# Retention and an ELU layer on one Trainium2 core: a new order for the opening, and input rows of 2 KB

## The chip, the cores and the metric

The kernel runs on one core of a Trainium2 chip. The metric is the time of one execution on the device, in microseconds (us), lower is better. The time is the median of several runs. One execution was also recorded by the hardware profiler; times "at" are counted from the start of its span.

Five engines work side by side, each through its own queue in order: TensorE (PE, with its weight loads as PEld), VectorE (DVE), ScalarE (ACT), GpSimd (POOL) and SyncE (SP), which here issues all transfers between HBM and the on-chip memory SBUF. TensorE writes into PSUM banks; VectorE and ScalarE read them.

## What is computed

A recurrent retention over four sequences of 768 tokens with 8 heads of 64, then a two-layer network with an ELU, in float32:

```python
B, H, S, D = 4, 8, 768, 64
gamma = 1.0 - 2.0 ** (-5.0 - np.arange(H))
for t in range(S):
    state = gamma[None, :, None, None] * state + np.einsum('bhd,bhe->bhde', k[:, :, t], v[:, :, t])
    y[:, :, t] = D ** -0.5 * np.einsum('bhd,bhde->bhe', q[:, :, t], state)
x = y.transpose(0, 2, 1, 3).reshape(3072, 512)
h = x @ w_in                                   # 512 x 2048
g = np.where(h > 0, h, np.exp(np.minimum(h, 0)) - 1)
out = g @ w_out                                # 2048 x 512
```

## The kernel before

**Tiling.** The 3072 tokens are cut into 24 chunks of 128, and four chunks make a block of 512 tokens. Six blocks are worked through. The retention of a chunk is done in halves of 64 tokens: scores of queries and keys, masked (`score_products`, L302; `mask_pair`, L324, or `scores`, L312, for two chunks together); the products of keys and values that make a state (`state_products`, L332; `state_sum`, L343); and the outputs from within the half (`within`, L389) and across from the state (`across`, L399), which VectorE multiplies with powers of gamma into `xb`, the input of the layer. `scale_v` (L275) multiplies the values with negative powers first, on VectorE or on GpSimd. All of these products are 64 x 64 and short.

**The layer on block 0** is plain: `plain_first` (L489) makes 16 tiles of 128 features x 512 tokens. A tile is four products of 128 x 128 weights with up to 512 tokens, two instructions each. `elu` (L472) follows: two activations on ScalarE and one last step on VectorE, which is put off until the next tile. Piece n of the weights feeds tiles 2n and 2n + 1. Later blocks use Strassen's scheme for both layers and are not touched.

**Weights** arrive as float64 bits, in pieces of 1 MB (`load_piece`, L126; three buffers). A piece is turned into float32 by ScalarE (`prepare`, L147: two or three activations for each part) and by VectorE (`decode`, L180: L190 in some pieces, L191 and L194 for each part). `decode` also loads the next piece when it ends. `hold` (L112) makes a load wait for another by a one-element copy on GpSimd.

**Order.** The schedule is written out by hand: the program order is each engine's order. Several steps are Python generators that are advanced piece by piece: `next(y)` runs the next step of a chunk's outputs, `next(inner)` the next part of a layer tile, `take()` the next decoding step of a weight piece. SP issues in the opening (L253 to L261): chunk 0 in two halves, half of weight piece 0, chunk 1, the other half, piece 1, chunks 2 and 3, and piece 2 held behind piece 1. TensorE begins with multiplications of zeros ("blank", L1108 to L1113, and `unread`, L1104) whose results nobody reads. Then come chunk 0, chunk 1 with the first 128 columns of tile 0 in between, the first halves (256 columns) of tiles 0 to 4, with chunks 2 and 3 taken together between them, the second halves of tiles 0 to 4, and whole tiles from tile 5 on (L1114 to L1171 and the loop at L1187). Within the loop the further pieces are prepared and decoded, the chunks of block 1 loaded, and at its step 4 four subtractions of outputs are made on VectorE (L540).

PSUM: banks "a" (two), "b" and "d" (one each) and four of pool `ps_r`. In `plain_first` tiles 0 to 3 take a, a, b, d, tile 4 one of `ps_r` (`hp`), and tiles from 5 on a, a, b, d in turn (L519).

**Rows of a transfer.** The arrays are laid out on the host. A chunk is 128 rows of 8 KB, one for each partition, and a weight piece too (4 KB for each of two halves):

```python
nc.sync.dma_start(t[:, c], qkv[m, :, c])
nc.sync.dma_start(t[:, c].rearrange("p c w -> p (c w)"), w_bits[n].bitcast(U32)[:, d])
```

## Time and profile before

| | |
|---|---|
| median of three runs | 633.58 us (633.03 to 634.15) |
| the profiled execution's own time | 632.87 us |
| its span in the profile | 630.9 us |
| TensorE busy | 624.8 us, 99% |
| VectorE busy | 483.1 us, 77% |
| ScalarE busy | 253.3 us, 40% |
| transfers | 136.85 MB, mean 217 GB/s |

A row of a timeline gives the start, the length, the engine, the line, the operation and the tiles (written, then read), the shapes and the number of instructions that the row merges; in brackets stands how long the engine was idle before it, and what released it. A row of a table by stretches gives the stretch, its length, the busy time of PE, PEld, DVE, ACT and POOL with instruction counts, the granted TensorE clock, the busy share of the DMA engines and the rate in GB/s. A busy TensorE is not always TensorE at its peak, since a waiting instruction can be counted as a long one.

### The profile page before, as it was taken

The numbers are of one execution on the slowest core, as the hardware profiler recorded it, in microseconds if no ns is written. First come the engines' busy times: TensorE is split into PE (matmuls) and PEld (weight loads), VectorE is DVE, ScalarE is ACT, GpSimd is POOL, SyncE is SP. The second block draws the span as 40 slices with busy tenths as digits, with TensorE's granted clock in tenths as the row PEclk, the third lists the DMA queues.
The fourth block names the chain that finished last, engine by engine and source line by source line (L and its number), as shares of the span: only waits on it lengthen the run. The fifth ranks groups of instructions, "written<-read, shape, count | busy, mean of one in ns | idle before, by whom it ended". The sixth has DMA issues, their size and how long they took to land.

```text
span 630.9 us, 16128 instructions
## 1 busy us (share of the span) xinstructions
PE 624.8 (99%) x6680; PEld 560.1 (89%) x6680; DVE 483.1 (77%) x884; ACT 253.3 (40%) x472; POOL 21.8 (3%) x25
## 2 busy tenths in 40 slices
PE   8999999999999999999999999999999999999998
PEld 5864578888899999889999989999988999988997
DVE  5779789989789675699685588777489877558975
ACT  6698635015541114653112646111465211366311
POOL 1021000000000000200000200000110000000000
PEclk9999999999999999999999999999999999999999
DMA  8698669689287888405888702888810798600794
GB/s 331 278 406 291 188 210 268 196 267 316 81 311 248 239 255 299 180 2 174 274 266 292 282 2 64 264 284 296 310 73 12 216 308 252 217 18 2 232 309 162
DMA packets 75897, 136.85 MB, mean 217 GB/s; under 512 B 6320, under 2 KB 31792, under 8 KB 70704
## 3 DMA queue, kind: packets, MB, share of 16 engines
q1 hardware_dynamic: 75824, 135.82, 64.8%
q8 instruction: 53, 0.87, 0.5%
q14 instruction: 20, 0.16, 0.1%
HBM read 114.56 MB, written 21.23 MB: 215 GB/s over the span
## 4 chain that ended last, share of the span: by engine, by line
PE 77%; SPq 1%; DVE 1%; DMA 1%; issue 0%; ACT 0%; ACTq 0%; DVEq 0%
PE pa L955 20%; PE pa L913 10%; PE pd L955 10%; PE pb L955 5%; PE pa L867 5%; PE pb L913 4%; PE pa L740 4%; PE qa L913 3%; PE pd L867 2%; PE qd L913 2%; PE pd L913 2%; PE pd L740 2%; PE y L394 1%; PE sc L307 1%; PE y L409 1%; PE kv L338 1%
## 5 line engine op out<-in xcount | busy, mean ns | idle before, releaser
L963 ACT COPY ms<-pa 128x128 f32<-128x128 f32 x104 | 27.7, 266 | 146.7 <-PE pa L955 146.7
L955 PE MATMUL pa<-ts,wq 128*128 128x128 f32 x560 | 74.2, 275 | 0.0
L955 PE MATMUL pd<-ts,wq 128*128 128x128 f32 x552 | 73.5, 276 | 0.0
L955 PEld LDWEIGHTS pa<-ts,wq 128*128 128x128 f32 x560 | 68.5, 192 | 0.4
L955 PEld LDWEIGHTS pd<-ts,wq 128*128 128x128 f32 x552 | 67.1, 192 | 0.6 <-DVE res L967 0.2
L955 PE MATMUL pa<-gC,wq 128*128 128x128 f32 x480 | 64.7, 278 | 0.0
L478 ACT ACTIVATE r<-r 128x512 f32<-128x512 f32 x96 | 60.5, 630 | 3.1
L955 PEld LDWEIGHTS pa<-gC,wq 128*128 128x128 f32 x480 | 59.0, 192 | 1.5 <-issue 0.3
L477 ACT ACTIVATE r<-gC 128x512 f32<-128x512 f32 x64 | 39.9, 624 | 32.4 <-DVE gC L921 32.4
L967 DVE TENSOR_TENSOR res<-pd,ms 128x128 f32<-128x128 f32 x68 | 19.5, 287 | 39.6 <-PE pd L955 38.4
L481 DVE SCALAR_TENSOR_TENSOR gC<-r,gC 128x512 f32<-128x512 f32 x64 | 44.0, 719 | 0.7 <-ACT r L478 0.7
L829 DVE TENSOR_TENSOR ts<-gC,ts 128x512 f32<-128x512 f32 x60 | 41.3, 688 | 1.0
L829 DVE TENSOR_TENSOR ts<-gC 128x512 f32<-128x512 f32 x60 | 41.0, 684 | 0.0
L281 POOL TENSOR_TENSOR chunk<-chunk,vf 128x512 f32<-128x512 f32 x16 | 20.0, 1251 | 428.8 <-DMA chunk<-in_qkv_dram 345.8
L955 PE MATMUL pb<-gC,wq 128*128 128x128 f32 x240 | 31.7, 275 | 0.0
L988 ACT COPY res<-pa 128x128 f32<-128x128 f32 x34 | 9.0, 266 | 55.0 <-PE pa L955 55.0
L955 PEld LDWEIGHTS pb<-gC,wq 128*128 128x128 f32 x240 | 29.2, 192 | 0.0
L690 ACT COPY m<-pa 128x512 f32<-128x512 f32 x24 | 13.9, 581 | 30.2 <-PE pa L740 16.3
L921 DVE TENSOR_TENSOR gC<-qa,gC 128x512 f32<-128x512 f32 x8 | 5.5, 692 | 25.0 <-PE qa L913 18.3
L913 PE MATMUL pa<-xt,w_b 128*128 128x256 f32 x96 | 23.0, 382 | 0.0
L913 PE MATMUL pa<-xt,w_s 128*128 128x256 f32 x96 | 23.0, 382 | 0.0
L913 PE MATMUL pa<-xb,w_a 128*128 128x256 f32 x96 | 22.7, 379 | 0.0
(255 smaller groups left out, 1244.3 us busy)
## 6 DMA issues: line engine op xcount, KB each, us to landing
wq<-scratch_dram SPq DMA_DIRECT2D x277, 256.0 KB, 4.3
chunk<-in_qkv_dram SPq DMA_DIRECT2D x23, 1024.0 KB, 8.6
wraw<-in_w_dram SPq DMA_DIRECT2D x15, 1024.0 KB, 6.0
out_dram<-res SPq DMA_DIRECT2D x14, 256.0 KB, 3.8
scratch_dram<-gT SPq DMA_DIRECT2D x12, 256.0 KB, 4.3
scratch_dram<-m SPq DMA_DIRECT2D x12, 192.0 KB, 6.0
scratch_dram<-so SPq DMA_DIRECT2D x4, 512.0 KB, 4.6
scratch_dram<-wi SPq DMA_DIRECT2D x2, 1024.0 KB, 6.4
```

The lines of the kernel that those rows point to most:

```text
L281: eng.tensor_tensor(out=kv[:, 1], in0=kv[:, 1], in1=vf[:, i].unsqueeze(2).to_broadcast([C, H, D]), op=ALU.mult)
L477: nc.scalar.activation(e, h, AF.Relu, scale=-1.0)
L478: nc.scalar.activation(e, e, AF.Exp, scale=-1.0)
L481: nc.vector.scalar_tensor_tensor(g, e, -1.0, h, ALU.add, ALU.max)
L690: nc.scalar.copy(m, ps)
L740: nc.tensor.matmul(ps[:, fi, :], lhsT=w[:, fi, j2, :], rhs=x[:, j2, :], start=(begin and fi == 0 and j2 == 0), stop=(j2 == 1), skip_group_ ...
L829: sub = lambda o, x, y: nc.vector.tensor_tensor(out=o, in0=x, in1=y, op=ALU.subtract)
L867: nc.tensor.matmul(ps[:, f, :], lhsT=lhs[f], rhs=xs[j][k], start=(begin and f == 0), stop=True, skip_group_check=True,)
L913: nc.tensor.matmul(ps[:, fi, :], lhsT=w[:, fi, j2, :], rhs=x[:, j2, :], start=(j in (1, 7) and fi == 0 and j2 == 0), stop=(j2 == 1), skip_ ...
L955: nc.tensor.matmul(ps, lhsT=w[:, f, :], rhs=ts[j][k][:, f, :], start=(begin and f == 0), stop=(f == 3), skip_group_check=True,)
L963: nc.scalar.copy(m, ps)
L967: nc.vector.tensor_tensor(out=o, in0=x, in1=y, op=ALU.add)
```

## The change

The opening is put into another order, and the layout of the two inputs and the way in which they are loaded are changed:

- Loads: chunk 0 (two halves), chunk 1, weight piece 0 (two halves), chunks 2 and 3, piece 1. Piece 2 is issued after chunk 3's values are scaled on GpSimd, and held behind piece 1.
- Each chunk and each weight piece is laid out in HBM as four blocks of 128 rows of 2 KB, here and in every later load; one transfer brings 4 x 128 rows (2 x 128 for a half).
- Chunks 0 and 1 are worked through before the first part of the layer. Chunks 2 and 3 are then done one by one, each with its own scores, masks, states and outputs, between parts of 128 columns of tiles 0 and 1. Only these two tiles are cut in parts; tiles from 2 on are whole, in banks b, d, a, a in turn.
- Two multiplications of blanks with 512 columns are taken out. The powers of the later tokens are made after both halves of piece 0 are prepared, not between them. In `prepare` the second and third activation change places; which pieces use L190 instead changes.

```diff
-            c = slice(part * 2048 // parts, (part + 1) * 2048 // parts)
-            nc.sync.dma_start(t[:, c], qkv[m, :, c])
+            j = slice(part * ROWS // parts, (part + 1) * ROWS // parts)
+            nc.sync.dma_start(t.rearrange("p (j c) -> p j c", j=ROWS)[:, j], qkv[m, j].rearrange("j p c -> p j c"))
...
             nc.scalar.activation(flat, lo, AF.Copy, scale=2.0**-29)
+            if not by_vector:
+                nc.scalar.activation(lo.bitcast(FP32), hi.bitcast(FP32), AF.Copy, scale=2.0**-112)
             top = dst.bitcast(F8).rearrange("p (c b) -> p c b", b=4)[:, c, 3]
             nc.scalar.activation(top, hi.bitcast(FP32), AF.Copy, scale=2.0**-120, saturate=False)
-            if not by_vector:
-                nc.scalar.activation(lo.bitcast(FP32), hi.bitcast(FP32), AF.Copy, scale=2.0**-112)
...
     load(0, 2)
-    parts = load_piece_parts(2)
-    next(parts)
     load(1)
-    next(parts, None)
-    load_piece()
+    load_piece(None, 2)
     load(2)
     load(3)
-    load_piece(staged[1][:, :, 0].bitcast(FP32))
+    load_piece()
...
+        for k in range(2):
+            banks.append(bank("a").rearrange("p a b -> p (a b)"))
+            for x in range(2):
+                part(k, slice(x * C, (x + 1) * C))
                 yield
+        for x in (2, 3):
+            for k in range(2):
+                part(k, slice(x * C, (x + 1) * C))
+                if x == 3:
+                    n, w, row, fi = tiles[k]
+                    elu(g_plain[row * NF + 2 * n + fi], banks[k])
                 yield
+        for k, (n, w, row, fi) in enumerate(tiles[2:]):
+            hp = bank("bdaa"[k % 4]).rearrange("p a b -> p (a b)")
```

The order of the opening after the change, from chunk 0's outputs on:

```python
    scale_v(3)
    load_piece(staged[1][:, :, 0].bitcast(FP32))
    ...
    for _ in range(4):
        next(y)
    score_products(sc, 0, 0, 1)
    prepare(2)
    piece = decode(True)
    state_sum(kvs, 0, 0, 0, 1)
    scale_v(1)
    mask_pair(sc, 0, 1)
    state_products(kvs, 0, 0, 1, range(2))
    state_sum(kvs, 0, 0, 1, 0)
    next(y)
    next(y)
    take()
    next(y)
    next(y)
    take()
    state_sum(kvs, 0, 0, 1, 1)
    powers_of(slice(2 * C, S))
    inner = plain_first()
    next(inner)
    sc = two("sc")
    score_products(sc, 0, 1, 0)
    scale_v(2, True)
    mask_pair(sc, 1, 0)
    next(inner)
    take(3)
    kvs = two("kv")
    state_products(kvs, 0, 1, 0, range(2))
    state_sum(kvs, 0, 1, 0, 0)
    y = outputs_of_first(1)
    next(y)
    next(inner)
    next(y)
    score_products(sc, 0, 1, 1)
    mask_pair(sc, 1, 1)
    next(y)
    next(inner)
    next(y)
    state_sum(kvs, 0, 1, 0, 1)
    prepare(2)
    piece = decode(True)
    state_products(kvs, 0, 1, 1, range(2))
    state_sum(kvs, 0, 1, 1, 0)
    next(y)
    next(inner)
    next(y)
    next(inner)
    next(y)
    next(y)
    state_sum(kvs, 0, 1, 1, 1)
    take(2)
```

In the loop over the rest of `plain_first`, step 0 now finishes the decoding of piece 1 and prepares piece 2, and steps 1 to 5, 7 and 9 each decode a piece and prepare the next:

```diff
-        if n in (1, 2, 4, 5, 7, 9):
-            next_piece(n in (1, 2, 5, 7))
+        if n == 0:
+            take(3)
+            prepare(2)
+        elif n in (1, 2, 3, 4, 5, 7, 9):
+            next_piece(n in (2, 3, 5, 7))
```

## The prediction

> **What bounds the kernel now.** I read the page first, then the timelines of TensorE, VectorE and GpSimd over the first 60 us, then stretches for the rates of the transfers. Times "at" are microseconds from the start of the span.
>
> ```profile
> PE 624.8 (99%) x6680; PEld 560.1 (89%) x6680; DVE 483.1 (77%) x884; ACT 253.3 (40%) x472; POOL 21.8 (3%) x25
> PE 77%; SPq 1%; DVE 1%; DMA 1%; issue 0%; ACT 0%; ACTq 0%; DVEq 0%
> ```
>
> TensorE is busy 624.8 of 630.9 us and holds the chain that ended last. From 60 us on it has no idle time, so the change is worth what it does to TensorE before that. The timeline of TensorE shows where the opening loses:
>
> ```profile
> 9.13 0.45 PE L409 MATMUL pd<-chunk 64*64 64x64 f32 x8 [0.26 <-DVE seen L426]
> 9.51 1.13 PE L1106 MATMUL pa<-blank 128*128 128x512 f32 x2
> 10.66 0.69 PE L307 MATMUL sc<-chunk 64*64 64x64 f32 x32
> 11.59 1.13 PE L497 MATMUL pa<-xb,w_a 128*128 128x128 f32 x8 [0.23 <-DVE w_a L194]
> 12.65 0.69 PE L338 MATMUL kv<-chunk 64*64 64x64 f32 x32
> ...
> 14.96 1.13 PE L1106 MATMUL pa<-blank 128*128 128x512 f32 x2
> 15.92 3.10 PE L497 MATMUL pa<-xb,w_a 128*128 128x128 f32 x16
> 18.93 1.99 PE L497 MATMUL pb<-xb,w_b 128*128 128x256 f32 x8
> 20.86 1.16 PE L307 MATMUL sc<-chunk 64*64 64x64 f32 x64
> ...
> 38.21 3.60 PE L521 MATMUL pa<-xb,w_a 128*128 128x512 f32 x8
> 41.65 3.60 PE L521 MATMUL pa<-xb,w_b 128*128 128x512 f32 x8
> ```
>
> Chunk 0 starts at 5.15 and its last products issue at 9.13 to 9.44. Chunk 1 starts only at 10.66, when it has landed. L1106 multiplies blanks: two such rows cover waits. At 38.21 all four chunks and tiles 0 to 4 of the layer are done. From there a tile takes 41.65 - 38.21 = 3.44 us. **38.21 is my yardstick**: whatever the changed kernel needs to reach the same state, plus waits after it, is the change in time. VectorE sets the pace of a chunk:
>
> ```profile
> 9.97 0.41 DVE L350 TENSOR_TENSOR chunk<-kv,chunk 128x256 f32<-128x256 f32 x1
> 10.75 0.69 DVE L194 CUSTOM_DVE_ANT_0 w_a<-wraw,w_a 128x1024 uint16<-128x1024 uint16 x1
> 13.38 0.42 DVE L350 TENSOR_TENSOR xt<-kv,chunk 128x256 f32<-128x256 f32 x1 [0.66 <-PE kv L338]
> 15.44 0.41 DVE L433 TENSOR_TENSOR xb<-pd,etab 128x256 f32<-128x256 f32 x1
> 43.71 1.94 DVE L194 CUSTOM_DVE_ANT_0 w_b<-wraw,w_b 128x2048 uint16<-128x2048 uint16 x1
> 48.34 0.68 DVE L481 SCALAR_TENSOR_TENSOR gC<-r,hp 128x512 f32<-128x512 f32 x1
> ```
>
> From the first state sum of chunk 1 (13.38) to the end of its last output (15.85) are 2.47 us of steps that wait for each other: sum, products, a 4-column read (L426), products, two scalings.
>
> **What the skill says.** (1) "SBUF — State Buffer", section "Who interferes with whom": VectorE and GpSimd share a port pair; a VectorE instruction with two SBUF inputs contends with a GpSimd one that reads SBUF, and whichever comes second waits for the whole instruction. The trace agrees at least in part: L194 at 43.71 took 1.94 us, the same shape takes 1.23 elsewhere, and GpSimd was in L281 from 43.01 to 44.57. (2) "TensorE: Matmul & The Clock Gate", section "Part 1: The HAM clock gate": the clock is halved after an idle window of about 3.4 us. Before, the granted clock is 1.00 in each stretch I asked for; no run here shows how much idling inside a window is allowed. (3) "DMA: Bandwidth & Descriptors", section "Why small descriptors are slow (HBM only)": about 3 cycles a packet on top of one per 32 bytes. That gives an estimate of 67/64 for 2 KB against 259/256 for 8 KB, 3.5% slower. The stretches below agree in sign: rows of 8 KB (first line) at 423 GB/s, fetches of wq in 2 KB rows (second) at 397, 6% less.
>
> ```profile
> 39.00:44.00 5.00, 5.00 (x13) 2.28 (x12) 2.57 (x5) 4.87 (x8) 1.57 (x2) 1.00 1.01 423
> 312.00:313.00 1.00, 1.00 (x11) 1.00 (x11) 1.00 (x3) 0.27 (x1) 0.00 (x0) 1.00 1.03 397
> ```
>
> **The change part by part.**
>
> *Loads.* Landings before, from what waits for them: chunk 0 at 6.4 (L281 starts 6.46), half of weight piece 0 at 8.1 (L164 starts 8.11), chunk 1 at 10.6 (L307). So 1 MB takes 2.5 us and half of it 1.7, or 1.3 when the stream is dense. In the new order, with 6% on each MB (2.65): chunk 1 at 9.1, piece 0 at 10.7 and 12.4, chunk 2 at 15.2, chunk 3 at 17.9, piece 1 at 20.5. Piece 2 is held by GpSimd until piece 1 is there, so the queue runs dry: before, a chunk issued at 30.66 on an idle queue was some 4.4 us under way, so piece 2 lands at about 25.1. VectorE needs piece 1 at 26, ScalarE piece 2 at 28: both covered. SP's issue of a load (0.44 us) may grow with four times the rows; even 1 us is hidden, since SP issues ahead of the stream.
>
> *Chunk 1.* Now at 9.1, so its scores run directly after chunk 0, at 9.45 instead of 10.66. VectorE: state sum 9.97 to 10.38, then L281 to 11.0 (no decoding between), the masks to 11.67; L338 at 11.05, state sum at 11.78. That is 1.6 us ahead of 13.38, so with the 2.47 from above the outputs end at 14.25.
>
> *Piece 0.* It lands 2.6 us later than before. Its first decode step (L191) falls between the 4-column reads and the outputs, at 12.9 (ScalarE has supplied it by 12.1 to 12.4: two activations of about 0.7 after 10.7; the swap of the second and third activation brings that forward 0.7). L194 follows the outputs, 14.2 to 14.9. Tile 0 begins 0.15 later, at 15.05, as 11.59 follows 11.44. The removed blanks (2 x 1.13) stood in waits and save nothing; the wait from 13.35 to 15.05 now stands open.
>
> *From 15.05: parts of tiles 0 and 1 between chunks 2 and 3.* A 128-column part is 8 instructions; at a quarter of 3.44 that is 0.86, but the part at 11.59 held TensorE 1.06 until L338 began. Likewise a 256-column part took 1.93 ahead of scores (18.93 to 20.86), against half of 3.44, 1.72. So a part followed by small products costs 0.2 more. A block of 32 small products takes 0.56, one of 16 takes 0.28. Six parts at 1.06, chunks 2 and 3 at 3 x 0.56 + 2 x 0.28 = 2.24 each, make 10.84; they end at 25.9. Inside it the second half of piece 0 must be decoded (L194 ends at 18.6, for a part due at 18.85: no wait). Then chunk 3's scaling: its second output ends at 26.85, so the part that reads it waits from 25.9 to 26.9. Two parts (1.72) end at 28.6, and tiles 2 to 4 (3 x 3.44) at **38.9**. Against 38.21: **+0.7**. All the gain of starting chunk 1 earlier goes into the open wait, the extra switches (six against three before) and the last wait.
>
> *GpSimd.* The scaling of chunk 3 (L281, mean 1.58 us there) moves from VectorE to GpSimd and starts as chunk 3 lands, 17.9, just when L194 of the second half (two SBUF inputs) is due at 17.9. If GpSimd is first, L194 ends up to 1.6 late and TensorE waits for it; if not, nothing. The one overlap before cost 0.7. I take **+0.6**, ends 0 and 1.6. Moving it off VectorE saves 0.6 there, in a spot with slack. The powers of the later tokens (2.55 us of ScalarE) move behind piece 0's second half: 15 to 17.6, needed at 21.4, covered.
>
> *Tile 8.* Before, tile 4 had a bank of its own (hp); now each tile from 6 on takes the bank of four tiles earlier. ScalarE has less prepared before the first elu (at 27): per tile 1.17 for the elu and 2.4 to 3.8 for the piece. Summed, tile 4's exponential ends at 45 and VectorE's four subtractions (L540, 2.8 us) stand ahead of its last step, which ends at 48.6 (before: 48.34 + 0.68). Tile 8 wants that bank at about 48.3 to 49.2. I take **+0.3**, ends 0 and 1.0. Later tiles have over 1 us of slack, and ScalarE catches up in its idle 2.4 us at 62.
>
> *Held ends for rows of 2 KB at the start*: chunk 0 comes at 165 GB/s in the first 5 us; smaller rows could make that better or worse by 0.5 in arrival. I take 0; ends -0.5 and +0.5. The later loads lie beside a full TensorE: 0.
>
> Sum: 0.7 + 0.6 + 0.3 = **+1.6 us**. On the profiled execution's own time, 632.87 (span 630.9, and 1.97 around it), that is 634.5. It lies 0.71 below the median of the three runs, 633.58; to that median I add the same difference: **635.2**. A measurement of this kernel can tell about 0.2% (1.27 us) from no change.
>
> **The rivals.**
>
> *Quick start, not slower.* If rows of 2 KB let chunk 0 come at the later rate of about 395 GB/s, its second half lands up to 1.3 earlier than 6.4. L281 of chunk 0 then starts when the scores allow the masks, about 0.85 earlier, and every step to tile 0 with it; chunk 3 lands early enough for GpSimd to be done before L194. Then +0.7 - 0.85 + 0.3 = +0.15: 633.7. It decides from 0.3 us of earlier landing. Against it: the first 5 us move only 165 GB/s because the queue has just begun, which small rows don't obviously mend.
>
> *Better packing, faster.* If the switches cost nothing in the new order (6 x 0.2 = 1.2 off) and the quick start holds (-0.85), with no wait at GpSimd or at tile 8: 0.7 - 1.2 - 0.85 = -1.35: 632.2. For it speaks that TensorE still has some 4 us of waits in its first 15 us to give; against it, that the 0.2 is seen at three places.
>
> *The clock gate.* Without blanks TensorE works 2.6 of the 5.6 us from 9.45 to 15.05. If that counts as idle, about 3.4 us run at half clock; some 1.7 of extra time on top of 0.7 + 0.6 + 0.3: +3.3, 636.9. Against: no gap is above 1.7 us.
>
> **How the numbers follow.** Forecast (+0.6 to +2.6 by its own ends, mostly above 1.27) 0.46; clock gate 0.09; quick start 0.29; better packing 0.16. So slower by over 0.2%: 0.46 + 0.09 = 0.55; within: 0.29; faster: 0.16. Range: from 632.2, the packing case, of which half lies below, to 637.0, a little above the clock gate. Left out: 0.08 below, some 0.06 above.
>
> **What would show it.** Right: scores of chunk 1 at about 9.5; an idle TensorE before tile 0 at about 15; the first 512-column tile at about 28.6 and the fourth (tile 5) at 38.9 or later; L281 of chunk 3 on GpSimd beside a long L194; a short wait ahead of tile 8. Wrong: chunk 0's L281 well before 6.4 (quick start); L497 parts that follow each other at 0.86 (packing); a granted clock under 1.00 (clock gate); waits for in_w_dram at ScalarE after 28 (loads too late).

## The result and the profile after

The changed kernel takes **644.4 us** (median of four runs, 642.97 to 644.96) against 633.31 (632.72 to 634.15) for the kernel before on the same chip: a ratio of 1.0168, 95% interval 1.0154 to 1.0182. It is slower by 11.1 us, where +1.6 was forecast. The profiled execution took 643.98, its span is 642.0.

The page of the changed kernel, its parts 1, 3 and 4:

```profile
PE 627.5 (98%) x6676; PEld 560.0 (87%) x6676; DVE 483.5 (75%) x887; ACT 253.7 (40%) x474; POOL 21.3 (3%) x26
...
q8 instruction: 53, 0.87, 0.5%
...
PE 88%; DMA 5%; DVE 3%; ACT 3%; issue 1%; SPq 0%; DVEq 0%
```

TensorE is still busy nearly all the time, and the chain's share of 88% for it, against 77% before, doesn't point to a loss: averages over the span don't show 11 us of 642. The best instrument is TensorE's matrix products, set side by side in program order with those of the kernel before, counted from the end: the difference of their start times is the **offset**, and each step in it is a place where time was lost. An offset comes from the one recorded execution of a kernel, a median from all its executions. A "product" is one MATMUL instruction of the profile. The yardstick of the prediction was the start of tile 5.

| place (time in the kernel before) | offset after it | step |
|---|---|---|
| start of tile 5 (38.21) | +6.43 | +6.43 |
| tile 8 (48.5) | +6.77 | +0.34 |
| states of block 1 (64.7 and 65.6) | +7.61 | +0.84 |
| first step after the tiles that asks for bank d (87.8) | +9.69 | +2.08 |
| 141 | +9.44 | -0.25 |
| a product that waits for a fetch of wq (178.9) | +11.08 | +1.64 |
| end | +11.07 | 0 |

TensorE's timeline of the changed kernel, from chunk 0's last products to tile 4 (start, length, line, tiles, count; in brackets the idle time before):

```profile
8.83 0.45 PE L401 MATMUL pd<-chunk 64*64 64x64 f32 x8 [0.26 <-DVE seen L419]
10.35 0.69 PE L299 MATMUL sc<-chunk 64*64 64x64 f32 x32 [1.07 <-DMA chunk<-in_qkv_dram]
11.07 0.56 PE L330 MATMUL kv<-chunk 64*64 64x64 f32 x19
12.94 0.59 PE L330 MATMUL kv<-chunk 64*64 64x64 f32 x11 [1.30 <-issue]
...
17.35 2.07 PE L488 MATMUL pa<-xb,w_a 128*128 128x128 f32 x8 [1.48 <-DVE w_a L189]
19.36 1.14 PE L299 MATMUL sc<-chunk 64*64 64x64 f32 x32
20.42 2.00 PE L488 MATMUL pa<-xb,w_a 128*128 128x128 f32 x8
22.35 0.69 PE L330 MATMUL kv<-chunk 64*64 64x64 f32 x32
...
32.45 2.05 PE L488 MATMUL pa<-xb,w_a 128*128 128x128 f32 x16 [0.88 <-DVE xb L425]
34.34 3.60 PE L508 MATMUL pb<-xb,w_b 128*128 128x512 f32 x8
```

Read three things. The state products of chunk 1 stop after 19 of 32 for 1.30 us, and the releaser is "issue": nothing that the profile shows was missing. A part of 128 columns at 17.35 lasts 2.07 where the same part lasts 1.16 later on. And tile 2 starts at 34.34, not at 28.6. The second thing is the clock. The table by stretches (busy PE, PEld, DVE, ACT, POOL, then the granted clock, the DMA share, GB/s):

```profile
10.00:15.00 5.00, 3.23 (x112) 2.76 (x112) 2.11 (x7) 3.33 (x6) 0.00 (x0) 0.70 1.05 392
15.00:20.00 5.00, 3.35 (x48) 2.94 (x52) 2.75 (x7) 2.91 (x5) 1.04 (x1) 0.50 0.88 326
20.00:25.00 5.00, 5.00 (x130) 4.54 (x126) 2.21 (x5) 3.55 (x6) 0.31 (x1) 0.78 0.48 108
```

The clock is at one half from 11.98 to 22.22, which is 10.24 us; before, it was 1.00 in all these stretches. The four executions of the changed kernel have a mean granted clock of 0.992 to 0.995, which makes some 6 to 10 us at one half in each (an estimate: twice the missing share of 642 us).

VectorE's timeline at chunk 1's first state sum, and at the decoding that tile 0 waits for:

```profile
13.55 0.42 DVE L342 TENSOR_TENSOR xt<-kv,chunk 128x256 f32<-128x256 f32 x1 [1.71 <-PE kv L330]
...
16.62 0.68 DVE L189 CUSTOM_DVE_ANT_0 w_a<-wraw,w_a 128x1024 uint16<-128x1024 uint16 x1
```

VectorE was idle for TensorE's stop, and the state sum comes at 13.55 where it came at 13.38 before: all that loading chunk 1 first had gained is gone by then.

The later step of 2.08 us is a wait of its own. TensorE's waits between 5 and 110 us, then VectorE's timeline at that place:

```profile
PE pd L598 <- DVE gC L472: 1.9, 1, 1.9
```

```profile
94.94 0.68 DVE L634 TENSOR_TENSOR gT<-gT,so 128x512 f32<-128x512 f32 x1
95.55 0.68 DVE L634 TENSOR_TENSOR gT<-so 128x512 f32<-128x512 f32 x1
96.15 0.68 DVE L634 TENSOR_TENSOR gT<-so,gT 128x512 f32<-128x512 f32 x1
96.75 0.68 DVE L472 SCALAR_TENSOR_TENSOR gC<-r,pd 128x512 f32<-128x512 f32 x1
```

Tile 15's last step (L472 at 96.75) reads bank d and stands behind three sums (L634) on VectorE. With tiles from 2 on in b, d, a, a, tile 15 comes to lie in d; before it lay in b. The next step of the kernel (`second_of_first`) asks for its banks in the order d, a, a, b, so d first.

### The profile page after: what moved, and what is told of

It reads as the page before. It is cut to its first block, busy times and chain, and to the rows that moved or that the text cites. A ratio compares the mean times of both kernels' runs of the same rounds, so it can differ in the third digit from the quotient of the medians.

```text
span 642.0 us, 16140 instructions
## 1 busy us (share of the span) xinstructions
PE 627.5 (98%) x6676; PEld 560.0 (87%) x6676; DVE 483.5 (75%) x887; ACT 253.7 (40%) x474; POOL 21.3 (3%) x26
## 4 chain that ended last, share of the span: by engine, by line
PE 88%; DMA 5%; DVE 3%; ACT 3%; issue 1%; SPq 0%; DVEq 0%
PE pa L942 20%; PE pa L900 10%; PE pd L942 10%; PE pb L942 5%; PE pa L854 5%; PE pb L900 4%; PE qa L900 3%; PE pa L727 3%; PE x L598 3%; PE pd L854 2%; PE qd L900 2%; PE pd L900 2%; PE pa L598 2%; PE kv L330 2%; DMA wraw<-in_w_dram 2%; PE y L386 2%
## 5 line engine op out<-in xcount | busy, mean ns | idle before, releaser
L942 PE MATMUL pa<-gC,wq 128*128 128x128 f32 x480 | 64.7, 278 | 1.5 <-DMA wq<-scratch_dram 1.5
L472 DVE SCALAR_TENSOR_TENSOR gC<-r,gC 128x512 f32<-128x512 f32 x64 | 45.3, 740 | 0.7 <-ACT r L469 0.7
L273 POOL TENSOR_TENSOR chunk<-chunk,vf 128x512 f32<-128x512 f32 x17 | 19.4, 1142 | 452.6 <-DMA chunk<-in_qkv_dram 429.9
L954 DVE TENSOR_TENSOR res<-res 128x512 f32<-128x512 f32 (+1 forms) x31 | 20.6, 666 | 3.0 <-DVE res L954 0.5
```

Of the source, the lines that this page charges most:

```text
L273: eng.tensor_tensor(out=kv[:, 1], in0=kv[:, 1], in1=vf[:, i].unsqueeze(2).to_broadcast([C, H, D]), op=ALU.mult)
L472: nc.vector.scalar_tensor_tensor(g, e, -1.0, h, ALU.add, ALU.max)
L942: nc.tensor.matmul(ps, lhsT=w[:, f, :], rhs=ts[j][k][:, f, :], start=(begin and f == 0), stop=(f == 3), skip_group_check=True,)
L954: nc.vector.tensor_tensor(out=o, in0=x, in1=y, op=ALU.add)
```

## The experiments

Two theories stood at the start. **Side costs**: the order itself is as cheap as the prediction had it (+0.7), and the rest is the halved clock, the rows of 2 KB and the bank of tile 15. **Order**: working off the chunks one by one costs by itself. In the texts of expectation, "the first kernel of this call" is the one with all side costs taken back (a_best), and "as measured above" is the kernel with chunk 1 first (b_c1first). All offsets below are at tile 5, against the kernel before. Where the mean granted clock of single executions is given, 0.997 stands for about 3.4 us at half clock, 0.995 for 7, 0.992 for 10 and 0.989 for 14 (estimated in the same way).

### The blanks, in both orders (a_blanks, b_noblank)

To the changed kernel the two stretches of 512 unread columns are given back (a_blanks); from the kernel before they are taken (b_noblank).

```diff
     for _ in range(4):
         next(y)
+    unread(1, TB)
     score_products(sc, 0, 0, 1)
...
     next(y)
+    unread(1, TB)
     next(y)
     take()
     state_sum(kvs, 0, 0, 1, 1)
```

> The changed kernel with the two removed multiplications of blanks (512 columns) put back, behind the outputs of chunk 0 and among those of chunk 1. Clock theory (the halved TensorE clock from 12.0 to 22.2 us comes from the missing blanks and costs 3 to 4 us): the granted clock stays 1.00 between 10 and 25 us, the first 512-column tile starts at about 31 instead of 34.3, and the time falls from 644.4 to about 641. Order theory (late weights and waits decide, the clock only fills waits): the clock may be whole, but the time stays within 1 us of 644.4. Rows theory: no change by this edit, 644.

Measured: 643.13 (642.09 to 645.13), ratio 1.0145 [1.0111, 1.0179]; offset +7.03. The clock is whole until 32.0 and then halved for 3.4 us.

> The kernel before with only its two multiplications of blanks with 512 columns in the opening taken out. Clock theory: the granted clock falls to about half for some microseconds after 12 us, and the time rises by 2 to 4 us, 635.5 to 637.5. Order and rows theories: the blanks stand in waits, the clock stays whole since TensorE has the first part of tile 0 at 11.6, and the time stays 633.3 within 0.5.

Measured: 635.84 against 633.85, ratio 1.0032 [1.0018, 1.0045]; half clock from 11.8 to 15.2, offset +0.78. So in the recorded executions the blanks hold the clock in the opening, in both orders. But half clock is a matter of chance: without the blanks, 8 of the 20 executions of b_noblank have a mean clock of 0.994 to 0.997 (median 637.3), and the other 12 have 0.999 or 1.0 (median 635.6); of the kernel before, 4 of 39 have 0.997. In the kernel before the blanks are worth some 2 us, and since the 12 with a whole clock lie 1.7 above it too, the clock is only part of that; the rest is not explained. In the changed kernel, giving the blanks back gains nothing that shows, and all four executions still have 0.994 to 0.997. Something takes the place of the half clock there: a stop of 1.35 us ("issue") at 30.2, which ends in half clock, and a long decoding step beside GpSimd:

```profile
18.98 1.31 DVE L189 CUSTOM_DVE_ANT_0 w_a<-wraw,w_a 128x1024 uint16<-128x1024 uint16 x1
```

```profile
18.50 1.25 POOL L273 TENSOR_TENSOR chunk<-chunk,vf 128x512 f32<-128x512 f32 x1 [16.23 <-DMA chunk<-in_qkv_dram]
```

L189 lasts 0.69 elsewhere; tile 0's next part waits 0.44 for it.

### The rows, in both orders (a_rows8, b_rows2)

```diff
-            j = slice(part * ROWS // parts, (part + 1) * ROWS // parts)
-            nc.sync.dma_start(t.rearrange("p (j c) -> p j c", j=ROWS)[:, j], qkv[m, j].rearrange("j p c -> p j c"))
+            c = slice(part * 2048 // parts, (part + 1) * 2048 // parts)
+            nc.sync.dma_start(t[:, c], qkv[m, :, c])
```

and the same for the weights and on the host (a_rows8; b_rows2 is the reverse, made to the kernel before).

> The changed kernel with the inputs laid out and loaded in rows of 8 KB as before (4 KB for halves), all else as changed. Rows theory (small rows delay every load and feed the late waits on weights): chunk 1 lands at about 9.2 instead of 10.3, weight piece 2 at about 25.5 instead of 27.1, the waits after 60 us shrink; about 641. Clock theory: the clock still drops, 643 to 644. Order theory: 643.5 to 644.5.

Measured: 642.03 (640.13 to 647.57), ratio 1.0114 [1.0069, 1.0159]; offset +6.05, half clock again from 12 to 22. That is the recorded execution, the slowest of the four (647.57, mean clock 0.987). Another has 0.989 and took 643.81; the other two kept the clock whole, without the blanks, and took 640.13 and 640.25. In one and the same kernel, half clock goes with 3.6 us or more.

> The kernel before with only the rows of 2 KB (layout and loads), its order kept. Rows theory: chunk 1 half a microsecond later and later loads 6% slower; 634.5 to 636. Clock and order theories: within 0.7 of the kernel before, 633.3.

Measured: 635.66 against 633.85, ratio 1.0032 [1.0017, 1.0047]; offset only +0.31, with a stop ("issue") of 0.37 at 29.24; a further 0.93 at block 1 and 1.5 at 299 us, a stop ("issue") again. The rows cost something in both orders, but in the changed order, as long as the clock is halved, hardly anything in the opening (+6.05 for +6.43).

### The later waits (a_bank, a_early)

```diff
-        X |= {j: bank(x) for j, x in ((7, "d"), (6, "a"), (5, "a"), (3, "b"))}
+        X |= {j: bank(x) for j, x in ((7, "b"), (6, "a"), (5, "a"), (3, "d"))}
```

> The changed kernel with one edit: in second_of_first, X[7] takes bank b and X[3] takes bank d (the reverse of the changed kernel). Bank theory: the 1.86 us wait of TensorE at 97.5 us of the changed kernel stands there only because X[7] asks first for bank d, which the new rotation has given to tile 15, whose last step comes late on VectorE. With the order turned round the wait goes, the offset against the kernel before falls by 1.9 to 2.1 at that place, and the median falls from 644.4 to about 642.4 (640.9 to 643.5). Rival, VectorE is behind there as a whole: the wait moves to X[6] or X[3] at its old length, and the median stays within 0.5 of 644.4.

Measured: 645.83 (643.74 to 653.25), ratio 1.021 [1.0149, 1.0272]. In its profile the wait is gone, and nothing waits in its place between 72 and 110 us. The granted clock was 0.95 from start to end in the profiled run, and the interval is 1.2% wide, so the median decides nothing here; the bank comes back below (a_best).

```diff
     state_sum(kvs, 0, 1, 1, 1)
-    take(2)
+    take(5)
+    prepare(2)
...
-        if n == 0:
-            take(3)
-            prepare(2)
-        elif n in (1, 2, 3, 4, 5, 7, 9):
-            next_piece(n in (2, 3, 5, 7))
+        if n in (0, 1, 2, 3, 4, 6, 8):
+            next_piece(n in (1, 2, 4, 6))
```

> The changed kernel with the whole of weight piece 1 decoded, and piece 2's preparation queued, ahead of the loop over the layer tiles, and every later piece one tile earlier, as the kernel before has it; the order of chunks, parts and tiles stays. Late-preparation theory: ScalarE's 8.3 us of idleness before tile 0's eviction and the late issue of the pieces' loads (piece 4 at 35.7 us) are what makes VectorE and ScalarE late at block 1 (0.85 us at 65 to 73 us) and at tile 15; then the offset added between 48 and 98 us falls from 3.3 to 0.5 to 1.5 us, and the median comes to 641 to 643.5. Rival, the lateness comes from the opening's order alone: the offsets after 48 us stay as they are, and the median stays at 643.5 to 645.5, or the earlier preparation delays tile 0 by 0.5 us and more.

Measured: 648.52 (647.64 to 650.08), ratio 1.0235 [1.0216, 1.0253]. The theory of late preparation falls: preparing earlier makes it worse by 4 us. TensorE's timeline of this kernel:

```profile
58.78 2.04 PE L508 MATMUL pa<-xb,w_a 128*128 128x512 f32 x3 [3.62 <-DVE gC L472]
```

Tile 8 now waits 3.62 us for bank a, because the decoding, and four subtractions behind it, stand ahead of tile 4's last step; and the clock is halved for 3.4 us right after. That is the wait the prediction put at +0.3, and it shows what sets it: what is queued ahead of the step that frees the bank.

### All the opening's side costs, and everything together (a_open, a_all)

a_open joins rows of 8 KB, the two blanks, and chunk 3 scaled on VectorE:

```diff
-    scale_v(3)
...
     score_products(sc, 0, 1, 1)
+    scale_v(3, True)
     mask_pair(sc, 1, 1)
```

> The changed kernel with three of its opening's costs taken back together: chunks and weights in rows of 8 KB, the two stretches of 512 unread columns back in front of chunk 0 and chunk 1, and chunk 3's values scaled on VectorE where its masks are drawn rather than on GpSimd beside piece 1. The order stays. If clock, late landing and the collision on SBUF make the opening's +6.4 us, the offset at tile 5 falls to +1 to +3 and the median to 639 to 641.5. Rival, the order itself costs it (the parts of tiles 0 and 1 in a row that waits for chunks, with fetch gaps of TensorE between): the offset stays at +5 or more, and the median at 642 or more.

Measured: 640.58 (639.27 to 641.23), ratio 1.0104 [1.0088, 1.012]; offset +3.83, and the clock whole throughout in the recorded execution (one of the four has 0.997). Between the two forecasts: some 2.6 us of the opening were side costs, 3.8 are left. At tile 8 it waits 0.7, at bank d 1.9.

> The edits of the three other kernels of this call together, so that of the change only the order stays (chunk 1 ahead of the weights, chunks 2 and 3 between parts of two tiles). If the causes are independent the gains add up: 635 to 638.5, within 1% of the kernel before. If the order itself is the cost: 640 to 642.5. Below 633 would show that the order is better than that of the kernel before once its side effects are gone; not expected.

Measured: 640.78 (639.76 to 641.87), ratio 1.0104 [1.0088, 1.0121]; offset +3.67. The wait at bank d is gone, but with the earlier preparation tile 8 waits 1.9 and half clock follows (1.7 us more). One edit's gain pays for the other's loss: the causes are not independent.

### The banks as before, and little left but the order (a_best)

a_open, and from tile 4 on the banks of the kernel before:

```diff
         for k, (n, w, row, fi) in enumerate(tiles[2:]):
-            hp = bank("bdaa"[k % 4]).rearrange("p a b -> p (a b)")
+            hp = ps_r.tile([P, 2, TH], FP32, name="hp", tag="r") if k == 2 else bank("bd aabdaabdaab"[k])
+            hp = hp.rearrange("p a b -> p (a b)")
```

> The changed kernel with its opening's side costs taken back (rows of 8 KB, the two stretches of 512 unread columns, chunk 3 scaled on VectorE) and with the banks of TensorE's results handed out as in the kernel before from tile 4 on: tile 4 gets a place of its own, the following ones a, a, b, d in turn. Of the change only the order stays. Bank theory: the waits for results still being read, 0.88 us at tile 8 and 2.14 at 95 us in the kernel without the second edit, both go, and the offset stays at the +3.8 that the opening leaves: 637.5 (636.5 to 638.5). Rival, VectorE is behind: the waits move on, 639.5 to 641.

Measured: 638.7 (637.71 to 640.98), ratio 1.0075 [1.0055, 1.0096]; offset +3.41, and no wait of TensorE between 42 and 110 us. The bank theory holds: both waits go and don't move on. But the order without these side costs is still slower than the kernel before. (Beside the order, the swap in `prepare` and the later preparation of the pieces are still in it; neither was tried alone in this kernel.)

### The order in two halves (b_c1first, b_inter)

b_c1first is the kernel before with chunk 1 loaded ahead of piece 0 and worked off before tile 0's first part:

```diff
-    parts = load_piece_parts(2)
-    next(parts)
     load(1)
-    next(parts, None)
+    for _ in load_piece_parts(2):
+        pass
     load_piece()
...
-    take()
-    take()
     scale_v(1)
     mask_pair(sc, 1)
     inner = plain_first()
-    next(inner)
     state_products(kvs, 0, 0, 1, range(2))
     state_sum(kvs, 0, 0, 1, 0)
     next(y)
     next(y)
+    take()
     next(y)
     unread(1, TB)
     next(y, None)
+    take()
+    next(inner)
     take()
     take()
     take()
```

> The kernel before with one part of the change: chunk 1 loaded ahead of piece 0 and worked off before tile 0's first part (which moves behind it, the powers of the later tokens behind piece 0's second half); chunks 2 and 3 stay a pair. In the changed kernel with its blanks back, tile 0 began at 16.07 with no part done; the kernel before has one part (1.06 us) done at 15.92. So if chunk 1 first costs what stood there, the offset at tile 5 is +1.2 and the time 634.8 (634.2 to 636). Rival, it gains as was meant, because only the interleaving of chunks 2 and 3 costs: 632.5 to 633.6.

Measured: 635.68 against 634.21, ratio 1.0021 [1.0007, 1.0035]; offset +0.21. The expectation of +1.2 failed: what chunk 1 first loses ahead of tile 0, three parts in a row (no switch between them) and quicker outputs of chunks 2 and 3 give back. It is about even in the opening. The median lies 1.5 higher all the same. The recorded execution (637.18) ends at +4.21: 1.9 were lost between 88 and 179 us, which was not followed up, and 2.1 in a stop at 303 us (below).

b_inter is the other half: chunk 1 as in the kernel before, chunks 2 and 3 one by one between the parts.

```diff
-    load(1)
-    load_piece(None, 2)
+    parts = load_piece_parts(2)
+    next(parts)
+    load(1)
+    next(parts, None)
     load(2)
...
     state_sum(kvs, 0, 0, 0, 1)
+    take(2)
     scale_v(1)
     mask_pair(sc, 0, 1)
+    inner = plain_first()
+    next(inner)
     state_products(kvs, 0, 0, 1, range(2))
...
-    inner = plain_first()
-    next(inner)
     sc = two("sc")
```

(against a_best; two `take()` later on are dropped with it).

> The opposite half: loads and chunk 1 as in the kernel before (half of piece 0 ahead of chunk 1, tile 0's first part between chunk 1's scores and states), then chunks 2 and 3 one by one between parts of tiles 0 and 1 as the change has it; rows of 8 KB, blanks, scaling on VectorE and the banks as before. If the two halves add up, the offset at tile 5 is 3.8 - 1.2 = +2.6 and the time 636.2 (635.2 to 637.2). Rival, the interleaving costs only because chunk 1 came first: within 1 of 633.6.

Measured: 639.16 (637.65 to 640.38), ratio 1.0075 [1.0058, 1.0092]; offset +3.90, of which 1.31 is a stop ("issue") at 19.08; without it some 2.6 would be left. So **taking chunks 2 and 3 one by one, between parts of two tiles, carries most of what the order costs**, whether chunk 1 comes first or not. TensorE's timelines show how; first b_c1first, then a_best, which begin tile 0 at the same time:

```profile
15.98 3.75 PE L496 MATMUL pa<-xb,w_a 128*128 128x128 f32 x24 [0.51 <-DVE w_a L194]
...
38.42 3.60 PE L520 MATMUL pa<-xb,w_a 128*128 128x512 f32 x8
```

```profile
15.92 1.16 PE L485 MATMUL pa<-xb,w_a 128*128 128x128 f32 x8 [0.42 <-DVE w_a L186]
...
22.33 0.27 PE L398 MATMUL pb<-chunk 64*64 64x64 f32 x2 [0.20 <-issue]
...
24.45 0.62 PE L327 MATMUL kv<-chunk 64*64 64x64 f32 x26 [0.32 <-DVE chunk L339]
...
29.44 2.05 PE L485 MATMUL pa<-xb,w_a 128*128 128x128 f32 x16 [0.85 <-DVE xb L422]
31.32 3.60 PE L506 MATMUL pb<-xb,w_b 128*128 128x512 f32 x8
...
41.63 3.60 PE L506 MATMUL pa<-xb,w_a 128*128 128x512 f32 x8
```

From there both have tiles 0 to 4 and chunks 2 and 3 to do. The pair needs 22.44 us, one by one needs 25.71. Summed by the starts of the rows: the layer parts 17.76 against 18.84 (six lone parts of 128 columns at 1.09 to 1.20, and two at 0.94), the products of the two chunks, short waits within them included, 4.68 against 6.01, and the wait of 0.85 at the end, which the pair doesn't have. Of the 1.3 more in the products, the ways back from small products to a part take 0.5 (six times 0.13 to 0.20, in the pair twice), and a stop for instructions 0.4 (at 22.33); the rest is spread. The wait for a chunk's sum (at 24.45) has its like in the pair, a wait of 0.32 for VectorE at 27.30. So VectorE's chains, which a pair might have covered, are 0.85 of the 3.3 us; 1.6 are changes between large and small products, in both directions.

### TensorE's stops without a releaser (a_fetch, b_fetch)

The stop of the changed kernel stands after product 223 of TensorE's program, counted from the first blank. So does that of each kernel that works off chunk 1 first. a_fetch is a_best with the 28 small blank multiplications of the start replaced by one of 384 columns. Each multiplication is two products in this count, so it is 54 products fewer, where the expectation reckoned with 27.

```diff
-    for n in range(28):
-        nc.tensor.matmul(
...
-        )
+    unread(1, 384)
```

> The first kernel of this call with the 28 small blank products of the start replaced by one of 384 columns, which lasts about as long (28 x 0.055 = 1.5 us at the half clock of the start) and is 27 products fewer. Fetch theory: TensorE's stop of 0.87 us after 17 of chunk 1's state products stands where its next 16 KB of instructions arrive, some 2.4 us after their transfer starts at 10.1; 27 products fewer ahead of it means that TensorE reaches that place 27 x 0.0175 = 0.47 us later, so the stop falls to about 0.4, in the middle of the products within the chunk, and the state sums of chunk 1 come about 0.9 us earlier. Rival, the stop belongs to the products themselves and stays at 0.8 to 0.9 behind the same product. Time 636.5 to 637.5 against 637.5.

Measured: 641.0 (638.97 to 644.36), ratio 1.0099 [1.0075, 1.0124]; offset +5.27. The stop moved, as the fetch theory says: it stands 54 products later in the work, again after product 223 of the count. But it is not shorter (12.66 to 14.05 between starts): the transfer came 1.6 us later too, at 11.56, and half clock for 3.4 us followed.

b_fetch goes the other way, on b_c1first: 64 small blanks in place of the stretch of 512 columns and 28 small ones (70 products more, where the expectation reckoned with 35), and no blank ahead of chunk 1.

```diff
-    unread(1, TB)
-    for n in range(28):
+    for n in range(64):
...
     next(y)
     next(y)
-    unread(1, TB)
     score_products(sc, 0, 0, 1)
```

> The kernel before with chunk 1 first, as measured above, with two edits: the 512-column blank and 28 small ones of the start become 64 small ones (35 products more, the same stretch of time), and the blank ahead of chunk 1 goes. Fetch theory: the stop comes whenever TensorE reaches product 223 of its program before the block that starts there has arrived, some 2.3 us after a transfer that begins around product 175 to 200. Product 223 is now old product 188, in the middle of chunk 1's scores, and its block is asked for around old 140, at 8 us: so the stop falls to between 0 and 0.6 us and stands inside the scores, the states of chunk 1 follow with no stop after 11.05, tile 0 starts at 15.1 to 15.5 rather than 15.98, and the offset at tile 5 goes from +0.2 to between -0.7 and -0.2: 633 to 635. Rival 1, the stop stays with the state products: no gain. Rival 2, without the blank the clock halves as in the kernel before without its blanks (+0.8): 634.5 to 636.

Measured: 641.87 (640.64 to 644.35), ratio 1.0131 [1.0111, 1.0152]; offset +4.90. TensorE's timeline:

```profile
9.60 0.27 PE L393 MATMUL pd<-chunk 64*64 64x64 f32 x2 [1.32 <-issue]
...
15.79 0.48 PE L408 MATMUL pd<-chunk,xt 64*64 64x64 f32 x3 [1.10 <-issue]
```

There are now two stops, after products 223 and 351, in quite other work than before (inside chunk 0, and in chunk 1's outputs), and with them 10 us of half clock. The count was forecast rightly; the place in the work was not, since 70 products move it out of chunk 1's scores and back into chunk 0, nor was the length. The page counts 53 transfers of 0.87 MB in all in the queue called "instruction"; the changed kernel's 6676 products and as many weight loads make 65 bytes each, so 16 KB hold about 126 products. The stops stand where such a block begins (in bold, the start after a stop; in b_fetch the second is after product 351):

| kernel | product 223: transfer starts; products before and after start | product 350 | product 605 |
|---|---|---|---|
| before | 10.31; 12.81, 12.82 | 16.39; 21.09, 21.10 | 26.36; 28.72, 28.93 |
| changed | 10.51; 11.41, **12.94** | 16.78; 22.36, 22.36 | 29.21; 32.45, 32.67 |
| a_best | 9.98; 11.28, **12.31** | 16.22; 18.30, 18.53 | 25.97; 28.32, 28.33 |
| a_best2k | 10.41; 10.96, **12.87** | 16.73; 18.86, **19.36** | 28.67; 29.30, **30.89** |
| b_inter | 10.35; 13.01, 13.02 | 16.53; 17.50, **19.08** | 26.46; 28.52, 28.75 |
| b_fetch | 7.12; 8.05, **9.60** | 13.37; 14.38, **15.79** | 28.26; 31.01, 31.02 |

After a stop with over half a microsecond of idle time in the opening TensorE goes on 2.2 to 2.6 us after the transfer began, in every recorded execution. Between the first two transfers lie 5.9 to 6.5 us. The kernel before reaches product 223 at 12.8 because a slow part of tile 0 lies ahead of it, and so never feels it. This is as near to shown as the records allow: the counts are fixed, the times follow the transfers, and two edits moved the stops by the products they took or added. What sets when a transfer starts stays open.

The same stop comes back late in six of the recorded executions. b_noblank, b_c1first, b_rows2, a_rows8, a_cold and a_early stop for 1.1 to 2.6 us after product 3258 or 3259, at 302 to 316 us, 21 blocks behind product 605, and go on 2.2 to 2.9 us after the transfer of that block began. In b_c1first it began at 301.23:

```profile
303.59 0.34 PE L408 MATMUL y<-chunk 64*64 64x64 f32 x5 [1.80 <-issue]
```

The kernel before reaches product 3259 at 299.38, 4.9 us after its transfer began, and does not stop.

### The clock, the rows and GpSimd, each alone (a_cold, a_best2k, a_gp)

Each takes one side cost back into a_best. a_cold leaves out the two blanks:

```diff
-    unread(1, TB)
     score_products(sc, 0, 0, 1)
...
-    unread(1, TB)
     next(y)
     take()
```

> The kernel with all side costs taken back (638.7), without its two stretches of 512 unread columns. Clock theory: the granted clock halves at about 12 us for some 10 us, as in the changed kernel; the parts and products of tile 0's first stretch last twice as long, and the offset at tile 5 rises from +3.4 to +5.5 to +6.2: 640.5 to 641.5. Rival, the time is set by chains of waits on VectorE and by the fetch of instructions, and the blank itself holds chunk 1 up by 1.1: the offset stays within 1 of +3.4.

Measured: 640.5 (639.44 to 645.94), ratio 1.0124 [1.0094, 1.0153]; offset +6.53. In this recorded execution the clock theory holds, at 3.1 us more than a_best. By stretches:

```profile
10.00:15.00 5.00, 3.04 (x98) 2.64 (x96) 2.69 (x9) 4.56 (x8) 0.00 (x0) 0.64 1.03 426
15.00:20.00 5.00, 3.52 (x53) 3.00 (x46) 2.35 (x6) 1.72 (x3) 0.00 (x0) 0.50 0.62 254
```

It is the slowest of the six (645.94, mean clock 0.989). Four others have 0.992 or 0.995 and took 639.44 to 641.93, and the one that kept its clock whole took 639.82. So the 3.1 us are read from one opening, and the times of these six don't single the clock out.

a_best2k has rows of 2 KB again (the edit of a_rows8 reversed).

> The kernel with all side costs taken back (638.7), with rows of 2 KB again. By the landings of the changed kernel against those of the kernel with rows of 8 KB (chunk 3 at 18.71 against 17.62, piece 1 at 21.30 against 20.06), transfers come 1.1 to 1.2 later, but nothing on the path waits for them: offset at tile 5 within 0.5 of +3.4, time 638.5 to 640. Rival, the rows cost 2 us as they did in the kernel before (635.66 against 633.85), by later waits of TensorE for instructions: 640 to 641.5.

Measured: 640.85 (638.77 to 645.53), ratio 1.0128 [1.0098, 1.0159]; offset +6.04. The rival was right: 2.6 us for the rows, and by stops, not by landings, in the one execution recorded. TensorE's waits between 8 and 48 us in this kernel:

```profile
PE pb L401 <- issue: 1.7, 2, 1.4
PE kv L330 <- issue: 1.7, 1, 1.7
```

In a_best these two are 0.2 and 0.8. The block at product 605 is asked for at 28.67 rather than 25.97; in a_blanks, which has the same rows, at 27.92.

a_gp scales chunk 3 on GpSimd again (the edit of a_open reversed).

> The kernel with all side costs taken back (638.7), with chunk 3's values scaled on GpSimd again, as the change has it, and not on VectorE. The prediction's term: L194 of piece 0's second half (L186 here) runs beside GpSimd and lasts 1.3 us rather than 0.69, tile 0's next part waits 0.4 to 0.6 for it, but VectorE's queue for chunk 3 gets 0.6 shorter, where TensorE waits for its state sum: offset +3.4 to +4.0, time 638.5 to 639.3. Rival, the shorter queue outweighs it: +2.8 to +3.3.

Measured: 637.35 (636.95 to 638.15), ratio 1.0063 [1.0048, 1.0079]; offset +3.45. No cost: with rows of 8 KB chunk 3 lands earlier, GpSimd is done (17.77 to 18.81) before the decoding step begins (19.23), and that step lasts 0.69. This is the best of the kernels with the new order, and it doesn't reach the kernel before, so there was no version that beats both.

## Why the prediction was wrong

The sign was right and named the likeliest, but the forecast of 635.2 and the upper end of 637.0 lie far below 644.4. By its own steps:

**Opening, +0.7 forecast, +6.43 measured: the step that failed.** Tile 0 was to start at 15.05 and started at 17.35 (+2.30). Chunk 1's first state sum ended its wait at 13.55, not at 11.78: the stop at product 223 held it to 12.94, and hid the later landing of chunk 1 (10.30 against 9.1 forecast; 9.2 in two other kernels with 2 KB rows, which stop at the same place). The steps from there to the outputs took 0.67 longer at half clock. From tile 0 to tile 2 were 13.55 us in the forecast and 16.99 in the trace (+3.44). Two parts and the scores between them lasted 5.00 in place of 2 x 1.06 + 0.56 = 2.68: half clock, 2.3 us. The rest, 1.1, is the products of chunks 2 and 3 (0.8) and the other parts (0.3). Tiles 2 to 4 took 3.44 each, as forecast. So of the 5.7 beyond the forecast half clock takes 3.0, the stop 1.6, and chunks and parts 1.1: the prediction let TensorE run at its full clock, with its instructions always there, and put both at nothing in its sum.

**The step inside it that stays wrong with clock and rows taken back (a_best)** is the count of "3 x 0.56 + 2 x 0.28" for a chunk, that is products at full pace, with only one wait, at the end. There the two chunks take 6.01, not 4.48, the eight parts 8.53, not 8.08; and tile 0 still starts at 15.92, since the stop at product 223 puts the state sum at 12.79. The trace gives names to the 1.5 in the chunks: the prediction counted the way from a part to small products (0.2 each, which was right: a lone part lasts 1.09) but not the way back, 0.13 to 0.20 six times, 0.9 in all; the stop for instructions after product 477 takes 0.4, and chunk 3's wait for its state sum 0.5 from start to start (between them the products ran a little faster than counted). The wait for VectorE that it did name, at the end, was 0.85 and not 1.0.

**The clock gate, a rival at 0.09 and +1.7.** It came, and in the recorded opening of the changed kernel it costs 3.0 us (3.1 in a_cold against a_best). The argument against it, "no gap is above 1.7 us", was no reason: the Trainium skill, "TensorE: Matmul & The Clock Gate", section "Part 1: The HAM clock gate", speaks of an idle window of some 3.4 us, and the lengths agree (half clock for 10.24, 6.83 and 3.41 us, multiples of 3.41). But here the clock fell at 11.98, and in the 3.41 us before it the idle times were 0.26, 1.07 and the first 0.34 of the stop, with work between them; in b_noblank 0.27 and 1.41 ahead of 11.8. In a_best2k TensorE stopped for 1.70 us at 11.2 to 12.9 and kept the clock. Over all the recorded executions TensorE was idle, by its recorded starts and ends, for 1.30 (a_cold) to 2.48 us (a_early) of the 3.41 before a fall within the program. So idle time well short of a whole window can suffice, against the page's wording; where the limit lies these runs don't settle. The clock first rose to full at 4.5 to 7.6 us and changed in steps of 3.41 from there, at other times in each execution, which may be why the same kernel falls in one and not in another. The forecast's 1.7 took some 3.4 us of half clock; it lasted 10.24.

**Stops for instructions: in no step of the prediction.** In the changed kernel the one at product 223 costs some 1.6 us. The profile of before gives no row for them, since its slow part lies in the right place.

**The gains of these removals don't add up**, which is why no single edit to the changed kernel helped much. In the recorded openings the clock costs 3.1 in a_cold and the rows 2.6 in a_best2k, each on top of the order's 3.4; the changed kernel, with both, is at 6.43, where the sum would be 9.1. At half clock TensorE reaches product 350 at 22.4 and product 605 at 32.4, when the blocks are there. Giving back the clock (a_blanks) brought the stop at 605 to light.

**GpSimd, +0.6.** In the changed kernel nothing: at half clock the decoding came at 21.77, long after GpSimd's 18.86 to 19.90. The collision itself is real (a_blanks: 1.31 for 0.69, a wait of 0.44), and agrees with the Trainium skill, "SBUF — State Buffer", section "Who interferes with whom", which says that a VectorE instruction with two SBUF inputs contends with a GpSimd one that reads SBUF. L273 took 1.04 to 1.25 there, not 1.58.

**Tile 8, +0.3.** Measured +0.34: right, mechanism and size, with the other edges of the same wait at 0.7 (a_open) and 3.6 (a_early).

**Rows of 2 KB, 0 at the start.** Chunk 0 landed 0.3 earlier (6.06 against 6.36; but 5.94 in b_noblank, with rows of 8 KB), inside the ends of this term, and TensorE then waited 1.07 for chunk 1; "the later loads lie beside a full TensorE: 0" was not, since rows changed when instructions come. So the quick start came at most in part and gained nothing, and the better packing did not occur.

**Bank d, +2.1: not foreseen.** The prediction said "later tiles have over 1 us of slack" and followed the banks only inside the loop over the tiles. The next user of bank d stands outside it.

**Not settled.** The 0.84 at block 1 (TensorE waits for VectorE's masks) appears with 0.66 to 1.24 in a_blanks, b_rows2 and a_best2k, not in a_best, a_open, a_gp; but also in a_cold (0.74), with rows of 8 KB, and not in a_early with 2 KB. The 1.64 at 178.9 appears in other kernels with 0.3 to 1.4 and in a_gp and a_open not at all; I take both for chance of a run, but that was not tried. The stops at 302 to 316 us in six other executions, which the recorded one of the changed kernel lacks, are stops for instructions (above); why that block's transfer begins late in them stays open. And a_best's median lies 1 us more above the kernel before than its offset of +3.41 at tile 5 says; 1.1 stand at 141 and 183 us of its profile.

## What to carry to other kernels

Before you reorder work on a full engine, ask of each new idle stretch what it does to the clock, count every change between large and small products, in both directions, and name what covers each wait for another engine: two chunks one by one, between parts of two tiles, cost 3.3 us more than as a pair, 1.6 of it in such changes and 0.85 in a wait for VectorE. When you change which tile uses which bank, follow the banks to their next user beyond the loop. Work whose results nobody reads can pay for itself by holding the clock; and if giving back one cost gains nothing, look for the next one that it had hidden before you call it harmless.

## What the runs showed of the hardware that was not expected

- TensorE stopped for up to 1.9 us in the opening, and up to 2.6 later (a_rows8, at 312.67), between two products with no releaser, always at the same counts of its program (223, 350 or 351, 477, 605, 3258 or 3259), some 127 products apart or a multiple of that, and went on 2.2 to 2.9 us after a 16 KB transfer on the instruction queue began. Small products (32 in 0.56 us) run through such a block in 2.2 us; the first two transfers lay 5.9 to 6.5 us apart in every kernel, while inputs were being loaded.
- With rows of 2 KB beside it, in the same order, the transfer for product 605 began 2.7 us later (28.67 against 25.97).
- The granted clock fell to one half after 3.41 us in which TensorE was idle for 1.30 to 2.48, and stayed there in multiples of 3.41 us, three of them while TensorE was 3.35 of 5 us busy. Once it was idle for 1.70 and the clock held (a_best2k). The same kernel did it in some executions and not in others (8 of 20 in b_noblank, 2 of 4 in a_rows8).
